# A fused attention and mixing kernel: two DMA transposes of 1024 columns for four of 512, in a new order of steps

## The chip, the cores and the metric

The kernel runs on one core of a Trainium2 chip. The core has a matrix engine (TensorE: PE in the profile, with its weight loads PEld), a vector engine (VectorE, DVE), a scalar engine (ScalarE, ACT), GpSimd (POOL) and SyncE (SP), which here only issues DMA transfers. The engines run side by side, each through its own list of instructions in order, and wait for each other through semaphores. PE writes its results to PSUM, which has eight banks of 128 partitions by 2 KB; DVE and ACT read them there.

The metric is the device time of one execution in microseconds (us), as the median over executions. A change under about half a per cent can't be told from none.

## The reference, cut to what matters

```
B, H, S, D = 8, 8, 576, 64        # q, k, v; factor 4
# attention on means of four neighbouring positions, repeated four times
q_d, k_d, v_d = means of 4 along S
out_up = repeat(softmax(q_d k_d^T / 8) v_d, 4)
# attention within a band: |i - j| < 4
out_local = softmax(where(band, q k^T / 8, -1e9)) v
x = (out_up + out_local), heads side by side: (8, 576, 512)
# mixing
theta = x @ w_theta
y = w_tok_r @ (x cos theta) + w_tok_i @ (x sin theta)      # along the 576 positions
u = x + y
out = u + relu(u @ w_ch)
```

Inputs and output are float32. The kernel computes in bfloat16 with float32 sums.

## The kernel before, in words

The eight batches go through the same chain of steps. Each step is a Python generator (`load`, `cast`, `turns`, ...), and each `yield` ends one piece of it. A string `ORDER` of 1178 letters says which generator is advanced next: `L` is the next piece of `load`, `C` of `cast`, `A` of `turns`, and so on, by the table `sequences` at the end of the kernel. This order fixes the order of the instructions on every engine (`pin` ties each instruction to the one before it on its engine). A second string, `BANKS`, names the PSUM bank of each result, and `ENGINES` the engine of each copy that may run on several (a = ACT, v = DVE, p = POOL). Nothing is scheduled at run time: an instruction whose input is late holds up all that stands behind it on its engine. SP's list holds all loads, all DMA transposes and most stores.

A piece is named here by its letter, batch and number: J1.0 is the first piece of `mix` of batch 1. Those that matter below:

- L, C: thirteen loads a batch into a ring of fifteen buffers `st` (four of k, four of q, five of v, each v piece in two transfers), and their casts to bfloat16. l, c: the twenty weight pieces (0 to 3 w_theta, 4 to 9 and 10 to 15 the two halves of w_tok_r and w_tok_i, 16 to 19 w_ch). V, v: w_tok turned on PE into `WT`, in eighteen pieces.
- A, a: q and k turned on PE; d, e: their sums over four positions; U, P, N, Q: pooled attention; S, m, O, i: banded attention; T, t: both added up into `xT`, x with channels on the partitions (`transposes_out`).
- H, h: theta and its cosines and sines (`phases`, `waves`), for positions 0 to 511 in four pieces. G, g, Z, z: the same for the last 64 positions, with a DMA transpose `z<-zT` at the end (`tail_z`).
- X: x turned back on PE, positions on the partitions (`x_turns`), for batches 0 to 5. M: the same by four DMA transposes of 128 x 512 (`x_turns_by_queue`), for batches 6 and 7 (`BY_QUEUE`), into a spare k buffer. y: the products x cos theta and x sin theta into `z` (`products`).
- J, j: the mix along positions, nine matmuls a piece, and u = x + y into `uT` and `ut` (`mix`, `mix_out`). For all but the first batch: four pieces of 512 positions and one of the last 64.
- R: u turned back by DMA transposes of 128 x 1024 (`residual`). K, b: the channel matmuls and the relu; D: stores. F, E, r, Y: these for the last 64 positions, two batches at a time.

Of the kernel before, what the change touches and what calls it, by code (L numbers as in the profile page):

```python
# [28 lines left out]
CH = 2 * STEP  # L29
NCH = 5  # L30
# [5 lines left out]
PG = CH // 4  # L36
KP = 32
HALF = 64

BY_QUEUE = [6, 7]  # L40
# [5 lines left out]
def kernel(  # L46
# [11 lines left out]
    nc = tc.nc  # L58
# [5 lines left out]


    ORDER = (
        "LkLkCLkLLLCLkCLACLkLkClkACLCCkaLlkAAaeCdkaaSedCkLSSsLPCsmLCOmsoPLkpCLOiopULOuoLuLLxicCxCONCNnLinlCno"
        "ClLAliATCnacmCCQAaLaAqOdatlocTSteeTLsXSsTLCidttmPPlcHcClTCptHOLLcHolpimOoHChlGhyCiXyhXUcLhLuuLOoLxiO"
        "yVxgvcoCCSNiLNnZnscLnCAXnQcamCCVOvoqlCCVVvvACcyTaelAVvtiVzVTaVvvltlcTtvAaTlHlTtVdLLdcLccSscCSsHvJVte"
        "LLVvLhVHvvXVyvChCJVvVVLCLvhLGXCvHyVVvXjjvghJjULLPPuZpCCyXuxLmJypJLOjjLOxSLooimCJLCljACsCiCaNnnNmAanC"  # L70
        "JAanQAqjLdOJOoLLLLzLeiajcToCStSTiCTOsLtSHtoLClsTimCHdstChJCCUlLCCjuAThAeutJLaLOaOLmlCjoPXopyCCiiJxjc"
        "OPLpLGcXyogHACiaxdhHNnLeZANhnnJnXLaSCSCysCjXcmCsQCyKKLURuRCKCqLeCdAuLaJLCOzLbxbjLSPsKALpbOoaiPLTLRbm"
        "CCtoJipTCxLAmCaCLNLTjtJnnTAjLNnTanLLJtttOSoJjQsOiCOGqJHCmjgLhoRHoDDiTjDXhCTiLHhCKCXtCeCAtayTZtKFXzCy"
        "yAHbUaRhLuOmoDHXuCHbRhiOyoiOLSDKsTJLteCHxdTChLdLKLKLbLtJoHLhejGiXDLhLjbXgDyCbAaJXmCCRCPSpdLKxLjybyJO"
        "OsPjJpCZCooAiNiaRzKCSsSCsDnnjbUDuKNdEbAunXLnKCCACyJraOaSemmQTbjqJCLTTxetLDCKsoiLOLDjPtpAbaxCJodLLiCt"
        "OOPooHRpDiimhDTNjtnnJmOOHToioKXijbhLCAXJyCayFHNtChCGgDjnXDnHKyQhbXUyuOZSKYqeuRTzxsoEitdJrPmSbJxTpjjs"
        "OotPpTTJitjtTtKJmbOjoDOSsDHoMNinHRNnRnMKnMGhbmQgihJqTOYoOTKMZDjtoHhDiitHyhTyytbTKyEHTFHztJtjMGhJgZjh"
        "MKHJHbMMzyJrKjjKDhbJyhyRKyYDRbJJDJJbjbJKDjjjDjFRjKKKRbDKKbRDbbbbDEKrDDDDbKbYDD"
    )
    BANKS = (  # L80
        "0246024602467206426014261401246250460267154202604624506102504523674230164267104570135732135143602456"
        "2046042607246074267046723450364260542054607240672401762304126416420106245162056245026754670154206704"
        "7203526043676452346730546025260402560423650436204673267402702460412604526301654012367403267406240376"
        "236042726023701247601234572016763274523410576452341076"
    )
    ENGINES = dict(
        C=(
            "aavvpvaavpppvappppapppvppppaapppppppappppappappapppappaapaapaappvppppapvaavaavpvpppppaapaaaaapvv"
            "papppapp"
        ),  # L90
        a="vvaaavaaaaaaaaaaavvaaaaaaaaaaaaa",
        c="vpapppppppppappppvpp",
        q="vvavaaav",
        u="vaavvavaaaavaaaa",
        v="vvvvavvavvavvavvva",
    )


# [30 lines left out]
    def tile_of(name, shape, dt=BF16):  # L129
        return const.tile(shape, dt, name=name)  # L130
# [109 lines left out]
    wth = tile_of("wth", [P, 4, DM])  # L240
# [24 lines left out]
    held = {}  # L265
# [262 lines left out]
    xTs, zs, css = {}, {}, {}  # L528

    def transposes(b):  # L530
        for c in range(NCH):
# [10 lines left out]
                    )  # L542
            yield

    def transposes_out(b):
        xdT = xds.pop(b)
        xT = xTs[b] = rot("xT", [P, 4, S], BF16, 2)
        for c in range(NCH):
            cnt = OWN[2 * c] + OWN[2 * c + 1]
            nc.vector.tensor_tensor(  # L550
                out=xT[:, :, CH * c:CH * c + cnt].rearrange("p e (m j) -> p e m j", j=4),
                in0=held.pop(("xT", b, c))[:, :, 0:cnt].rearrange("p e (m j) -> p e m j", j=4),
                in1=xdT[:, :, PG * c:PG * c + cnt // 4].unsqueeze(3).to_broadcast([P, 4, cnt // 4, 4]),
                op=ALU.add,
            )
            yield

    def phases(b):  # L560
        xT = xTs[b]
        for c in range(4):
            th = held["th", b, c] = one()
            for dc in range(4):
                nc.tensor.matmul(out=th, lhsT=xT[:, dc, P * c:P * c + P], rhs=wth[:, dc, :], start=(dc == 0), stop=(dc == 3))  # L565
            yield
# [9 lines left out]
    csts, zTs = {}, {}  # L576

    def tail_phases(b):
        xT = xTs[b]
        th = held["tt", b] = one()[:, 0:4 * HALF].rearrange("p (e t) -> p e t", e=4)  # L580
        for ec in range(4):
            for dc in range(4):
                nc.tensor.matmul(out=th[:, ec, :], lhsT=wth[:, dc, P * ec:P * ec + P], rhs=xT[:, dc, 512:576],
                                 start=(dc == 0), stop=(dc == 3))
        yield

# [7 lines left out]
    def z_of(b):  # L594
        if b not in zs:
            zs[b] = rot("z", [P, 9, DM], BF16, 2)
        return zs[b]

    def tail_product(b):
        zT = zTs[b] = rot("zT", [P, 4, 2, HALF], BF16, 1)  # L600
        nc.vector.tensor_tensor(
            out=zT, in0=xTs[b][:, :, 512:576].unsqueeze(2).to_broadcast([P, 4, 2, HALF]), in1=csts.pop(b), op=ALU.mult,
        )
        yield

# [4 lines left out]
        yield  # L610

    def x_turns(b):
        xT = xTs[b]
        for c in range(4):
            ps = held["xt", b, c] = one(BF16)[:, 0:DM]
            for dc in range(4):
                nc.tensor.transpose(out=ps[:, P * dc:P * dc + P], in_=xT[:, dc, P * c:P * c + P], identity=ident)  # L617
            yield

    xms = {}  # L620

    def x_turns_by_queue(b):
        spare = rot("k_tm", [P, 2, WR, 2, D], BF16, 2).rearrange("p i r c d -> p (i r c d)")
        xm = xms[b] = spare[:, 0:4 * DM].rearrange("p (c n) -> p c n", c=4)
        for dc in range(4):
            nc.sync.dma_start_transpose(out=xm[:, :, P * dc:P * dc + P], in_=xTs[b][:, dc, 0:512])
            yield

    def products(b):
        for c in range(4):  # L630
            x = xms[b][:, c, :] if b in BY_QUEUE else held.pop(("xt", b, c))
            nc.vector.tensor_tensor(  # L632
                out=z_of(b)[:, 2 * c:2 * c + 2, :], in0=x.unsqueeze(1).to_broadcast([P, 2, DM]),
                in1=css.pop((b, c)), op=ALU.mult,
            )
            yield

# [6 lines left out]
    def pieces(b):  # L644
        if b in BY_HALF:
            return [(dc, 288 * hf, 288) for hf in range(2) for dc in range(4)]
        whole, tail = [(dc, 0, 512) for dc in range(4)], [(None, 512, HALF)]
        return tail + whole if b == B - 1 else whole + tail
# [9 lines left out]
            yield  # L658

    def mix_out(b):  # L660
        xT = xTs[b]
        uT = uTs[b] = rot("uT", [P, 6, S], BF16, 2).rearrange("p a s -> p (a s)")[:, 0:4 * DM].rearrange("p (e t) -> p e t", e=4)
        if b % 2 == 0:
            uts[b // 2] = rot("ut", [P, 4, 2, HALF], BF16, 2)
        ut = uts[b // 2][:, :, b % 2, :]
        for dc, lo, n in pieces(b):
            ps = held.pop(("u", b, dc, lo))
            if dc is None:
                nc.vector.tensor_tensor(out=ut, in0=ps[:, 0:4 * n].rearrange("p (e t) -> p e t", e=4), in1=xT[:, :, lo:], op=ALU.add)
            else:  # L670
                m = min(512 - lo, n)
                nc.vector.tensor_tensor(out=uT[:, dc, lo:lo + m], in0=ps[:, 0:m], in1=xT[:, dc, lo:lo + m], op=ALU.add)  # L672
                if m < n:
                    nc.vector.tensor_tensor(out=ut[:, dc, :], in0=ps[:, m:n], in1=xT[:, dc, 512:], op=ALU.add)
            yield

    def residual(b):
# [78 lines left out]
    def each(steps, n=B):  # L756
# [57 lines left out]
```

## Time and profile before

| What | us |
|---|---|
| median of three executions | 245.51 |
| lowest, highest | 245.32, 246.25 |
| the profiled execution's own time | 243.21 |
| span of its instructions | 241.5 |

The 40 slices of the page show the busy share of each engine in tenths. In the start PE is the least busy of the four, and the DMA engines are full; from about the eleventh slice (60 us) PE is at 9 nearly throughout; the loads end near the 28th.

```profile
PE   1457878798999799999999999999998998999992
PEld 1344745586687356666665466565754474446441
DVE  1698999885799799989888898999977877657463
ACT  4183689679989789865789498746684174330000
POOL 1588986677475746640066412191410000000000
PEclk9999999889999999999999999999999999999999
DMA  6999999999998998999999999998662187349576
```

A busy PE is not PE at its peak: short matmuls and a lower granted clock stretch it. PEclk is the clock that was granted, in tenths.

### The profile page before, as it was taken

Reading aid. Unit: us, or ns where it says so; the run is one execution under the profiler, and the core shown is the slowest. Engines: PE = TensorE matmul, PEld = TensorE weight load, DVE = VectorE, ACT = ScalarE, POOL = GpSimd, SP = SyncE. Lnnn points to the kernel's source line nnn. Section 1 sums busy time; section 2 is a strip of 40 time slices with the busy share of each in tenths; the row PEclk is TensorE's granted clock in tenths of the full one; section 3 lists DMA queues with packets and bytes.
Section 4 is the critical chain, followed back from the end, with each engine's and each line's share of the span. In section 5 each row is a group of like instructions: output and inputs, shape, how many; then the busy total and the mean of one; then the engine's idle time right before and its main releaser. Section 6 shows DMA issues by size and latency. Waiting matters only on the chain.

```text
span 241.5 us, 8125 instructions
## 1 busy us (share of the span) xinstructions
PE 213.1 (88%) x3307; PEld 135.0 (56%) x3344; DVE 194.1 (80%) x385; ACT 150.5 (62%) x218; POOL 93.4 (39%) x165
## 2 busy tenths in 40 slices
PE   1457878798999799999999999999998998999992
PEld 1344745586687356666665466565754474446441
DVE  1698999885799799989888898999977877657463
ACT  4183689679989789865789498746684174330000
POOL 1588986677475746640066412191410000000000
PEclk9999999889999999999999999999999999999999
DMA  6999999999998998999999999998662187349576
GB/s 201 270 222 297 274 187 271 338 220 160 282 259 194 310 273 184 233 267 155 270 274 230 223 251 222 274 240 217 156 83 78 24 132 177 68 103 244 130 227 213
DMA packets 87190, 50.91 MB, mean 211 GB/s; under 512 B 72048, under 2 KB 72304, under 8 KB 87152
## 3 DMA queue, kind: packets, MB, share of 16 engines
q1 hardware_dynamic: 86640, 49.60, 89.8%
q10 hardware_dynamic: 512, 0.79, 0.9%
q8 instruction: 26, 0.43, 0.8%
q14 instruction: 12, 0.10, 0.1%
HBM read 34.11 MB, written 9.44 MB: 180 GB/s over the span
## 4 chain that ended last, share of the span: by engine, by line
PE 61%; DMA 13%; DVE 10%; issue 4%; ACT 4%; SPq 4%; POOL 3%; DVEq 0%; ACTq 0%; POOLq 0%
PE space L656 25%; PE space L699 10%; PE space L565 6%; DMA st<-in_k_dram 4%; PE space L298 4%; DMA st<-in_moe_w_tok_i_dram 3%; PE space L498 3%; DMA st<-in_q_dram 2%; DVE kd L315 2%; PE space L538 2%; PE space L617 2%; DMA z<-zT 2%; PE space L412 2%; PE space L466 1%; PE space L418 1%
## 5 line engine op out<-in xcount | busy, mean ns | idle before, releaser
L656 PE MATMUL space<-WT,z 128*128 128x64 bf16 (+2 forms) x561 | 76.4, 284 | 3.2 <-DMA z<-zT 1.7
L656 PEld LDWEIGHTS <-z 128*128 128x128 bf16 x576 | 38.6, 98 | 31.6 <-DMA z<-zT 2.7
L672 DVE TENSOR_TENSOR uT<-space,xT 128x512 bf16<-128x512 f32 (+2 forms) x36 | 22.5, 626 | 12.6 <-PE space L656 12.3
L565 PE MATMUL space<-wth,xT 128*128 128x512 bf16 x115 | 31.1, 380 | 1.1 <-issue 0.3
L699 PE MATMUL space<-wch,uT 128*128 128x512 bf16 (+1 forms) x124 | 30.8, 372 | 0.5 <-issue 0.2
L572 ACT ACTIVATE cs<-space,pihc 128x512 bf16<-128x512 f32 x32 | 22.2, 695 | 13.5 <-PE space L565 9.5
L518 DVE TENSOR_TENSOR tmp<-space,rl 128x512 bf16<-128x512 f32 x40 | 26.9, 680 | 1.4 <-PE space L538 0.9
L125 POOL CAST k_tm<-st 128x576 bf16<-128x576 f32 x19 | 14.0, 739 | 34.8 <-DMA st<-in_k_dram 34.7
L550 DVE TENSOR_TENSOR xT<-space,xdT 128x464 bf16<-128x464 f32 (+1 forms) x40 | 24.4, 627 | 2.4 <-PE space L538 2.3
L478 ACT ACTIVATE pm<-space 128x1024 bf16<-128x1024 f32 (+1 forms) x24 | 20.5, 881 | 9.2 <-PE space L466 8.7
L315 DVE TENSOR_REDUCE kd<-kT 128x290 bf16<-128x1160 bf16 x16 | 21.4, 1350 | 0.0
L713 DVE SCALAR_TENSOR_TENSOR osb<-space,ur 128x512 f32<-128x512 f32 x28 | 19.0, 684 | 2.3 <-PE space L699 1.3
L125 POOL CAST v_w<-st 128x512 bf16<-128x512 f32 x21 | 13.6, 656 | 16.7 <-DMA st<-in_v_dram 14.4
L573 ACT ACTIVATE cs<-space 128x512 bf16<-128x512 f32 x32 | 19.3, 603 | 0.0
L298 PE MATMUL space<-ident,k_tm 128*128 128x128 bf16 x144 | 12.6, 241 | 7.4 <-ACT k_tm L125 5.9
L399 ACT ACTIVATE pd<-space 128x864 bf16<-128x864 f32 (+1 forms) x16 | 12.2, 771 | 10.5 <-PE space L380 6.4
L699 PEld LDWEIGHTS <-uT 128*128 128x128 bf16 x132 | 12.0, 98 | 11.5 <-issue 0.5
L125 POOL CAST q_tm<-st 128x576 bf16<-128x576 f32 x18 | 12.5, 702 | 15.0 <-DMA st<-in_q_dram 14.1
L332 POOL TENSOR_TENSOR two<-qT 128x576 f32<-128x576 bf16 x14 | 16.6, 1188 | 3.5 <-ACT qT L125 3.2
L632 DVE TENSOR_TENSOR z<-space,cs 128x1024 bf16<-128x1024 bf16 x24 | 16.2, 681 | 2.1 <-ACT cs L573 1.2
L125 ACT COPY kT<-space 128x1152 bf16<-128x1152 bf16 x14 | 15.7, 1122 | 3.1 <-PE space L298 3.1
L125 ACT COPY qT<-space 128x1152 bf16<-128x1152 bf16 x13 | 14.6, 1125 | 4.2 <-PE space L298 3.9
(95 smaller groups left out, 376.2 us busy)
## 6 DMA issues: line engine op xcount, KB each, us to landing
st<-in_v_dram SPq DMA_DIRECT2D x80, 128.0 KB, 5.3
st<-in_k_dram SPq DMA_DIRECT2D x32, 288.0 KB, 5.5
st<-in_q_dram SPq DMA_DIRECT2D x32, 288.0 KB, 5.6
out_dram<-osb SPq DMA_DIRECT2D x28, 256.0 KB, 4.4
st<-in_moe_w_tok_r_dram SPq DMA_DIRECT2D x6, 216.0 KB, 6.3
st<-in_moe_w_tok_i_dram SPq DMA_DIRECT2D x6, 216.0 KB, 7.1
st<-in_moe_w_theta_dram SPq DMA_DIRECT2D x4, 256.0 KB, 6.4
st<-in_moe_w_ch_dram SPq DMA_DIRECT2D x4, 256.0 KB, 5.3
```

The costliest lines, as they stand in the source:

```text
L125: copies[next(engines[step])](**operands)
L298: nc.tensor.transpose(out=ps[:, P * r:P * r + P], in_=(k_tm if what == "k" else q_tm)[:, i, r, :, :], identity=ident)
L315: nc.vector.tensor_reduce(out=kd[:, hs, :, 0:PG].rearrange("p e g m -> p (e g) m"), axis=AX.X, op=ALU.add, in_=kT[:, hs, :].rearrange("p e ...
L478: nc.scalar.activation(out=pm.rearrange("p e c j w -> p e (c j w)"), in_=held.pop(("S", b, u))[:, :, 0:4 * W * n], func=AF.Exp, scale=SCL)
L518: nc.vector.tensor_tensor(out=tmp.rearrange("p g (j d) -> p g j d", d=D), in0=held.pop(("loc", b, c))[:, :, :, 0:D], in1=rls.pop((b, c)).u ...
L550: nc.vector.tensor_tensor(out=xT[:, :, CH * c:CH * c + cnt].rearrange("p e (m j) -> p e m j", j=4), in0=held.pop(("xT", b, c))[:, :, 0:cnt ...
L565: nc.tensor.matmul(out=th, lhsT=xT[:, dc, P * c:P * c + P], rhs=wth[:, dc, :], start=(dc == 0), stop=(dc == 3))
L572: nc.scalar.activation(out=cs[:, 0, :], in_=th, func=AF.Sin, bias=pihc, scale=1.0)
L573: nc.scalar.activation(out=cs[:, 1, :], in_=th, func=AF.Sin, bias=0.0, scale=1.0)
L656: nc.tensor.matmul(out=ps[:, n * i:n * i + n], lhsT=z[:, j, P * d:P * d + P], rhs=WT[:, j, lo:lo + n], start=(j == 0), stop=(j == 8))
L672: nc.vector.tensor_tensor(out=uT[:, dc, lo:lo + m], in0=ps[:, 0:m], in1=xT[:, dc, lo:lo + m], op=ALU.add)
L699: nc.tensor.matmul(out=ps, lhsT=uT[:, dc, P * c:P * c + P], rhs=wch[:, dc, cols], start=(dc == 0), stop=(dc == 3))
```

## The change: a dense xT for batches 6 and 7, two transfers for four, and a new order

`xT` becomes a pair of views, made by a new function `x_of`. For batches 6 and 7 the first 512 positions of the four channel groups lie densely behind each other, followed by the last 64 of each; for the others the tile is as before and the views are slices of it. Two channel groups can then go through one DMA transpose of 128 x 1024, so `x_turns_by_queue` issues two where it issued four. The result lies by channel group first, so the products read it, and are written, through views with a channel group and 128 columns apart. The last piece of `transposes_out` of these two batches is split at position 512 into two additions. `ORDER`, `BANKS` and `ENGINES` are replaced as a whole: 1174 letters, four M pieces fewer, the same other pieces.

```
+    def x_of(b):
+        t = rot("xT", [P, 4 * S], BF16, 2)
+        if b in BY_QUEUE:
+            return [t[:, 4 * i:4 * i + 4 * n].rearrange("p (e t) -> p e t", e=4) for i, n in ((0, DM), (DM, HALF))]
+        t = t.rearrange("p (e t) -> p e t", e=4)
+        return [t[:, :, 0:DM], t[:, :, DM:], t]
+
     def transposes_out(b):
         xdT = xds.pop(b)
-        xT = xTs[b] = rot("xT", [P, 4, S], BF16, 2)
+        xTs[b] = x_of(b)
         for c in range(NCH):
             cnt = OWN[2 * c] + OWN[2 * c + 1]
...
+            for i, lo, n in [(0, CH * c, cnt)] if c < NCH - 1 else [(0, CH * c, DM - CH * c), (1, 0, HALF)] if b in BY_QUEUE else [(2, CH * c, cnt)]:
...
     def x_turns_by_queue(b):
         spare = rot("k_tm", [P, 2, WR, 2, D], BF16, 2).rearrange("p i r c d -> p (i r c d)")
-        xm = xms[b] = spare[:, 0:4 * DM].rearrange("p (c n) -> p c n", c=4)
-        for dc in range(4):
-            nc.sync.dma_start_transpose(out=xm[:, :, P * dc:P * dc + P], in_=xTs[b][:, dc, 0:512])
+        xm = xms[b] = spare[:, 0:4 * DM].rearrange("p (e c n) -> p e c n", e=4, c=4)
+        for dc in (0, 2):
+            nc.sync.dma_start_transpose(out=xm[:, dc:dc + 2].rearrange("p e c n -> p (e c) n"),
+                                        in_=xTs[b][0][:, dc:dc + 2, :].rearrange("p e t -> p (e t)"))
             yield
 
     def products(b):
         for c in range(4):
-            x = xms[b][:, c, :] if b in BY_QUEUE else held.pop(("xt", b, c))
+            x = xms[b][:, :, c, :] if b in BY_QUEUE else held.pop(("xt", b, c)).rearrange("p (e n) -> p e n", n=P)
             nc.vector.tensor_tensor(
-                out=z_of(b)[:, 2 * c:2 * c + 2, :], in0=x.unsqueeze(1).to_broadcast([P, 2, DM]),
-                in1=css.pop((b, c)), op=ALU.mult,
+                out=z_of(b)[:, 2 * c:2 * c + 2, :].rearrange("p r (e n) -> p r e n", n=P),
+                in0=x.unsqueeze(1).to_broadcast([P, 2, 4, P]),
+                in1=css.pop((b, c)).rearrange("p r (e n) -> p r e n", n=P), op=ALU.mult,
             )
             yield
```

Two stretches of the order, with the letters of the list above. The part in which w_tok is loaded (l), cast (c) and turned (V), and the mix of batch 0 (J) begins, before and after:

```
before  ...datlocTSteeTLsXSsTLCidttmPPlcHcClTCptHOLLcHolpimOoHChlGhyCiXyhXUcLhLuuLOoLxiOyVxgvcoCCSNiLNnZnscLnCAXnQcamCCVOvoqlCCVVvv...
after   ...qtCATlAtLaOtdelaSeToLSciltsscCXLLPLCPCLHmpplhTOLCtOoLmcHCHoiCLCyihlOUOLGLLhugouxxiAaXNcoHClZNnnyXnCCclylnhXSiysQCCqCAlcAcTAatVTlLcvl...
```

and the last steps:

```
before  ...jjjDjFRjKKKRbDKKbRDbbbbDEKrDDDDbKbYDD
after   ...DjDDjRFJjJbjYJJjKEjDKRKKKbKRrbKbRbbbDYDDKbDDDDbD
```

On the engines, `ENGINES` moves copies: of the eight first casts of k and q of batch 0 two q and one k leave DVE for POOL and ACT. ACT's list has eighteen table loads where it had sixteen: the steps that use the exponential and those that use the sine alternate once more.

More of the change, by code (lines that the diff above doesn't have):

```diff
@@ L543, in transposes @@
             yield
+    def x_of(b):
[4 more added lines that the diff above has]
+        return [t[:, :, 0:DM], t[:, :, DM:], t]
     def transposes_out(b):
         xdT = xds.pop(b)
-        xT = xTs[b] = rot("xT", [P, 4, S], BF16, 2)
+        xTs[b] = x_of(b)
         for c in range(NCH):
             cnt = OWN[2 * c] + OWN[2 * c + 1]
[L550 to L555, printed above, removed]
+            ps = held.pop(("xT", b, c))
+            for i, lo, n in [(0, CH * c, cnt)] if c < NCH - 1 else [(0, CH * c, DM - CH * c), (1, 0, HALF)] if b in BY_QUEUE else [(2, CH * c, cnt)]:
+                at = lo + DM * (i == 1) - CH * c
+                nc.vector.tensor_tensor(
+                    out=xTs[b][i][:, :, lo:lo + n].rearrange("p e (m j) -> p e m j", j=4),
+                    in0=ps[:, :, at:at + n].rearrange("p e (m j) -> p e m j", j=4),
+                    in1=xdT[:, :, (CH * c + at) // 4:(CH * c + at + n) // 4].unsqueeze(3).to_broadcast([P, 4, n // 4, 4]),
+                    op=ALU.add,
+                )
             yield
     def phases(b):
-        xT = xTs[b]
+        xT = xTs[b][0]
         for c in range(4):
@@ L582, in tail_phases @@
             for dc in range(4):
-                nc.tensor.matmul(out=th[:, ec, :], lhsT=wth[:, dc, P * ec:P * ec + P], rhs=xT[:, dc, 512:576],
+                nc.tensor.matmul(out=th[:, ec, :], lhsT=wth[:, dc, P * ec:P * ec + P], rhs=xt[:, dc, :],
                                  start=(dc == 0), stop=(dc == 3))
@@ L601, in tail_product @@
         nc.vector.tensor_tensor(
-            out=zT, in0=xTs[b][:, :, 512:576].unsqueeze(2).to_broadcast([P, 4, 2, HALF]), in1=csts.pop(b), op=ALU.mult,
+            out=zT, in0=xTs[b][1].unsqueeze(2).to_broadcast([P, 4, 2, HALF]), in1=csts.pop(b), op=ALU.mult,
         )
@@ L668, in mix_out @@
             if dc is None:
-                nc.vector.tensor_tensor(out=ut, in0=ps[:, 0:4 * n].rearrange("p (e t) -> p e t", e=4), in1=xT[:, :, lo:], op=ALU.add)
+                nc.vector.tensor_tensor(out=ut, in0=ps[:, 0:4 * n].rearrange("p (e t) -> p e t", e=4), in1=xt, op=ALU.add)
             else:
@@ L673, in mix_out @@
                 if m < n:
-                    nc.vector.tensor_tensor(out=ut[:, dc, :], in0=ps[:, m:n], in1=xT[:, dc, 512:], op=ALU.add)
+                    nc.vector.tensor_tensor(out=ut[:, dc, :], in0=ps[:, m:n], in1=xt[:, dc, :], op=ALU.add)
             yield
```

52 lines of the change are left out of this document (26 added, 26 removed).

## The prediction

> **What bounds the kernel now.** I read the page first: which engine is full, and where.
>
> ```profile
> span 241.5 us, 8125 instructions
> PE 213.1 (88%) x3307; PEld 135.0 (56%) x3344; DVE 194.1 (80%) x385; ACT 150.5 (62%) x218; POOL 93.4 (39%) x165
> ```
>
> PE is the fullest engine, with 28.4 us idle. The view by stretches says where; its columns are start:end, length, then busy us and instructions of PE, PEld, DVE, ACT and POOL, the granted clock, the DMA share and GB/s.
>
> ```profile
> 0.00:20.00 20.00, 7.11 (x146) 5.46 (x148) 12.87 (x37) 9.09 (x11) 10.20 (x47) 1.00 0.93 234
> 20.00:40.00 20.00, 17.51 (x355) 11.82 (x346) 18.47 (x37) 14.70 (x21) 16.32 (x26) 1.00 1.09 255
> 40.00:46.00 6.00, 4.25 (x99) 3.27 (x95) 5.09 (x14) 4.83 (x9) 3.76 (x7) 1.00 1.04 325
> 46.00:50.00 4.00, 3.43 (x51) 3.27 (x51) 3.07 (x9) 2.40 (x3) 2.66 (x4) 0.59 1.31 253
> 50.00:60.00 10.00, 9.18 (x168) 6.87 (x168) 7.28 (x15) 9.00 (x13) 7.78 (x11) 0.99 1.01 195
> ...
> 100.00:120.00 20.00, 19.74 (x376) 13.23 (x381) 17.67 (x36) 12.96 (x18) 5.30 (x8) 1.00 1.20 225
> ...
> 200.00:210.00 10.00, 8.76 (x63) 4.51 (x63) 7.21 (x13) 4.00 (x8) 0.00 (x0) 1.00 0.61 134
> ```
>
> Until 60 us the DMA engines are full (shares 0.93 to 1.31) and PE starves. Behind that PE hardly idles. The timeline of PE after 62 us (start, length, work, and in brackets the idle time before it and what ended it) has these waits of more than 0.3 us, and no others:
>
> ```profile
> 82.31 0.39 PE L656 MATMUL space<-WT,z 128*128 128x512 bf16 x1 [1.06 <-DMA z<-zT]
> 84.25 0.68 PE L298 MATMUL space<-ident,q_tm 128*128 128x128 bf16 x9 [0.33 <-ACT q_tm L125]
> 182.76 0.39 PE L656 MATMUL space<-WT,z 128*128 128x512 bf16 x1 [0.66 <-DMA z<-zT]
> 205.69 0.36 PE L538 MATMUL space<-ident,tmp 128*128 128x116 bf16 x4 [1.19 <-DVE xT L550]
> ```
>
> They add up to 3.24 us, which caps what any new order can win behind the start. The fourth belongs to the step that the change rewrites: DVE could not take the next xT because it stood before a product, waiting for x turned by DMA. SP's timeline and the group's idle time show it:
>
> ```profile
> 190.84 1.86 SPq L626 DMA_TRANSPOSE k_tm<-xT  x1
> 195.49 2.58 SPq L626 DMA_TRANSPOSE k_tm<-xT  x2
> 200.26 1.29 SPq L626 DMA_TRANSPOSE k_tm<-xT  x1
> L632 DVE TENSOR_TENSOR z<-k_tm,cs 128x1024 bf16<-128x1024 bf16 x8 | 5.2, 686 | 4.3 <-DMA k_tm<-xT 2.9 <-issue 1.4
> ```
>
> **The yardstick for the new order.** The order is written out, so each step has a place: the PE work that stands ahead of it, summed with the prices of the chain of waits (start, us, work):
>
> ```profile
> 131.34 0.21 PE space L538 x4
> 131.55 1.94 PE space L656 x9
> 133.49 0.86 PE space L565 x4
> 139.09 0.47 PE space L583 x16
> 140.00 0.50 PE space L298 x9
> ```
>
> and likewise for the rest; both orders hold 206.9 us of it, the same matmuls. Three places show how far PE lags behind its work: work 22.6 (V0.4) at 49.59 us, 27.8 (J0.0) at 55.36, 34.5 (J0.2) at 62.28. The lag is 27.0, 27.6, 27.8 us, and from there constant: the start decides 28 of the 34.6 us that the span has over the work (241.5 - 206.9), and what a change does to the lag at about 60 us it does to the end, but for the four waits.
>
> ```profile
> 49.59 0.81 PE L274 MATMUL space<-ident,uT 96*128 96x96 bf16 x9
> 55.36 1.26 PE L656 MATMUL space<-WT,z 128*128 128x288 bf16 x9 [0.72 <-ACT pm L478]
> 62.28 1.26 PE L656 MATMUL space<-WT,z 128*128 128x288 bf16 x9
> ```
>
> **The change part by part.** *Two transfers for four.* Issues of L626 (four of 512 columns) and of the residual's 1024-column form, from the tile views; then the medians to landing:
>
> ```profile
> L626 SPq DMA_TRANSPOSE k_tm<-xT x8: 1192/1268/2277, 190.8 to 213.0; - x8
> L681 SPq DMA_TRANSPOSE ur<-uT x17: 1188/1384/2742, 95.3 to 231.0; - x17
> ur<-uT SPq DMA_TRANSPOSE x17, 4.5
> k_tm<-xT SPq DMA_TRANSPOSE x8, 3.4
> ```
>
> SP spends 4 x 1.27 = 5.1 us on a batch now and 2 x 1.38 = 2.8 us then. Each transfer lands later (4.5 for 3.4 us), but in the new order the last one for batch 6 stands at PE work 168.4 and its first product at 176.7: 8.3 us for 4.5. Before, 170.9 and 172.6: 1.7 us for 3.4. In SP's queue it is behind two stores whose relu is done by then. So the 2.9 us of DVE's wait goes, and PE's 1.19 us. Given back in part: between T7.3 and J6.0 stand 4.3 us of PE work plus six matmuls (1.3), and DVE has there three xT pieces, two relus and four products, nine operations of 0.63 to 0.69 and one more of 0.42 for the split piece, 6.2 us less what they overlap: some 0.5 us. Net -0.7; bounds -1.19 and +0.5 (the wait stays in another form).
>
> *The split last piece* of xT, for two batches: 48 and 64 columns of four rows (192 and 256 elements) instead of 112. The nearest forms are 224 and 256 elements of L672 and L669, so at most 0.42 us of DVE is added to each batch; it is in the sum above. *The products' views* now have four dimensions, for all batches. L601 has such a view already:
>
> ```profile
> L672 DVE TENSOR_TENSOR uT<-space,xT 128x224 bf16<-128x224 f32 x4 | 1.6, 388 | 0.1
> L669 DVE TENSOR_TENSOR ut<-space,xT 128x256 bf16<-128x256 f32 x7 | 2.9, 418 | 1.0 <-PE space L656 1.0
> ...
> L601 DVE TENSOR_TENSOR zT<-xT,cst 128x512 bf16<-128x512 bf16 x8 | 3.5, 442 | 0.6 <-ACT cst L591 0.6
> L486 DVE TENSOR_TENSOR pm<-pm,band 128x512 bf16<-128x512 bf16 x8 | 3.3, 415 | 0.6 <-ACT pm L478 0.6
> L518 DVE TENSOR_TENSOR tmp<-space,rl 128x512 bf16<-128x512 f32 x40 | 26.9, 680 | 1.4 <-PE space L538 0.9
> ```
>
> L601 takes 0.03 us more than L486's flat form of its size: 32 x 0.03 = 1 us of DVE at most, spread over a DVE with 47 us idle: nothing. The far bound, the rate of L518 (512 elements in 680 ns), would be +0.65 us for each of 32, 21 us of DVE.
>
> *The order, at the start.* More first casts go to POOL and ACT, DVE has two q casts and one k cast fewer (0.75 us each, below), and copies kT out before its last memsets. The reduces that hold up the first pooled scores then start some 2 us sooner. I price that gain at nothing, because a DMA stands behind it: V0.1 to V0.8 need w_tok pieces 4 to 9, and the new order loads six more pieces of k and q of batch 2 ahead of them.
>
> ```profile
> L125 DVE CAST q_tm<-st 128x576 bf16<-128x576 f32 x4 | 3.0, 749 | 5.8 <-DMA st<-in_q_dram 5.8
> ```
>
> ```profile
> 38.59 0.61 POOL L125 CAST v_w<-st 128x512 bf16<-128x512 f32 x1 [0.81 <-DMA st<-in_v_dram]
> ...
> 44.00 1.27 POOL L125 CAST uT<-st 96x576 bf16<-96x576 f32 x2 [1.02 <-DMA st<-in_moe_w_tok_i_dram]
> 50.10 0.67 POOL L125 CAST q_tm<-st 128x576 bf16<-128x576 f32 x1 [0.46 <-DMA st<-in_q_dram]
> 55.51 1.27 POOL L125 CAST uT<-st 96x576 bf16<-96x576 f32 x2 [0.34 <-DMA st<-in_moe_w_tok_i_dram]
> ```
>
> Before, those six landed by 50.1 and the tok pieces by 44.6; the set is the same, so now the tok piece is last, at about 50.1, is cast by 50.8, and V0.1 (work 22.5) cannot start earlier: lag 28.3, against 27.0 at the same work. The second gate: V0.10 (work 31.1) needs the last tok piece, which landed at about 56.1 and now stands behind two more pieces of v. One is 256 KB at the 195 GB/s of that stretch, 1.34 us: 58.8, cast by 59.5, lag 28.4 against 27.7. The gates say +1.3 and +0.7; I take +1.0. Bounds: -2 (the early gain arrives whole) and +2.5 (POOL casts three pieces of batch 2 first).
>
> *The order, behind it.* z of batch 1: its transfer had landed 1.06 us late; its product moves from work 36.8 to 33.8, seven loads fewer are ahead of it in SP's queue, and J1.0 moves only from 51.4 to 49.7: -1.06. The q turn at 84.25 (A4.0, A4.1) moves from 53.9 and 54.6 to 55.1 and 60.6, so its loads have 1 to 6 us more: -0.33. z of batch 5: more distance (147.4 to 151.5) but a residual transfer and a store ahead of it: 0. ACT gets two more table loads (sin, exp and back in batches 3 and 4), 1.28 us each by the row below; ACT is idle for 7 us between 100 and 120 us: 0, at most +1.3.
>
> ```profile
> L478 ACT ACT_TABLE_LOAD x4 | 5.1, 1283 | 0.2
> ```
>
> *The end.* R7's three transfers still hang on the last pieces of uT, and the last relus and stores are the same: 0.
>
> **The sum.** 243.21 us is the profiled execution's own time (span 241.5). 243.21 + 1.0 - 1.06 - 0.33 - 0.7 = 242.1. The median shown is 2.3 above that execution: **244.4 us**, 0.4% faster. Half a per cent, 1.2 us, is about what a measurement here can tell from no change.
>
> **The rivals.** *The gates don't bind* (start 0 or better) and all four waits go: 245.5 - 3.24 = 242.3. For: DVE's freed time at the start. Against: DMA shares of 1.0 all the way to 60 us.
>
> *Slower: the clock falls at the gate.* PE's granted clock was 0.59 from 46 to 50 us, after six us at 71% busy (4.25 of 6.00): 4 x 0.41 = 1.6 us. The new order leaves 7.0 us of work between U1.0 (15.5, which needs the v piece that landed by 38.6, cast 0.6 later at 39.2, or some 0.5 sooner with one load fewer ahead) and V0.1 (at 50.8), so PE is some 58% busy there (7.0 of 12.1). A second such fall behind the gate, with the gate at its upper bound and the whole gain on the waits (2.1): 245.5 + 2.5 + 1.6 - 2.1 = 247.5. It makes the kernel slower once gate and clock cost over 2.1 us together. The Trainium skill, page "TensorE: Matmul & The Clock Gate", section "What's actually happening", says that the clock is halved after an idle window of about 3.4 us. By that rule alone PE would have to stand still to lose its clock; this trace lost it with no such gap, so the trace disagrees and the rival is likelier than the rule makes it.
>
> *No change:* the waits go and others of their size come, 245.5.
>
> *Slower: the products lose their rate*, 21 us of DVE, of which DVE's 47 idle us hide perhaps half: 255. L601 speaks against it.
>
> **How the numbers follow.** Forecast 0.45 (its own range 243.2 to 245.6; 0.20 of it below 244.3), gates don't bind 0.18, no change 0.07, clock at the gate 0.25, slow products 0.05. Faster by over 0.5%: 0.20 + 0.18 = 0.38; within: 0.25 + 0.07 = 0.32; slower: 0.30. The range 241.3 to 248.5 leaves out the slow products and the edges of two rivals.
>
> **What would show it.** Right: no wait of DVE on k_tm<-xT; SP issues of some 1.4 us, four in all; PE's first wait for WT's pieces near 50 us; no z wait at J1.0. Wrong: J0.0 starting before 55 us (the gates were no gates) or after 58.5; a granted clock under 0.8 past 52 us; products over 0.75 us; new waits of PE behind 62 us of more than 2 us in sum.

## The result, and the profile after

| | changed kernel | kernel before, same chip | ratio, 95% interval |
|---|---|---|---|
| first comparison, median | 242.25 us (4 executions) | 245.47 us (4) | 0.9857 [0.9828, 0.9886] |
| once more, median | 243.09 us (12) | 245.48 us (29) | 0.9907 [0.987, 0.9944] |
| profiled execution, own time | 241.83 us | 243.21 us | |
| its span | 240.1 us | 241.5 us | |

The change makes the kernel faster, by 1.4% in the first comparison and 0.9% in the second, where 0.4% was forecast. Between the profiled executions it is 1.4 us. The ratios leave out executions that were disturbed.

The head of the page, and the view by stretches (columns as in the prediction: busy us and instructions of PE, PEld, DVE, ACT, POOL, the clock, the DMA share, GB/s):

```profile
span 240.1 us, 8125 instructions
PE 211.8 (88%) x3311; PEld 134.9 (56%) x3344; DVE 195.2 (81%) x381; ACT 153.7 (64%) x222; POOL 95.6 (40%) x169
```

```profile
46.00:50.00 4.00, 1.90 (x33) 1.57 (x30) 2.93 (x6) 1.83 (x3) 2.42 (x4) 1.00 1.07 233
50.00:52.00 2.00, 1.12 (x18) 0.85 (x22) 1.37 (x3) 1.24 (x4) 1.63 (x4) 0.88 1.27 212
52.00:54.00 2.00, 2.00 (x87) 1.78 (x87) 1.45 (x3) 1.33 (x5) 1.92 (x3) 0.50 1.06 247
54.00:56.00 2.00, 1.95 (x27) 1.27 (x19) 1.26 (x2) 1.85 (x3) 2.00 (x4) 0.77 1.50 181
...
100.00:140.00 40.00, 38.58 (x559) 23.48 (x566) 36.36 (x65) 32.81 (x46) 13.99 (x21) 1.00 1.14 240
```

PE is busy 1.90 of the 4 us from 46 to 50, where it had 3.43 before: it waits for loads. The clock then falls to 0.50, later than before (46 to 50 us). PE's timeline shows the waits, and POOL's what ends them (in brackets the idle time and what ended it):

```profile
48.76 0.68 PE L298 MATMUL space<-ident,q_tm 128*128 128x128 bf16 x9 [1.93 <-POOL q_tm L125]
49.28 0.29 PE L274 MATMUL space<-ident,uT 96*128 96x96 bf16 x3
49.41 0.37 PE L538 MATMUL space<-ident,tmp 128*128 128x116 bf16 x4
49.62 0.21 PE L274 MATMUL space<-ident,uT 96*128 96x96 bf16 x1
50.29 0.22 PE L274 MATMUL space<-ident,uT 96*128 96x96 bf16 x1 [0.47 <-POOL uT L125]
51.10 0.90 PE L274 MATMUL space<-ident,uT 96*128 96x96 bf16 x13 [0.59 <-POOL uT L125]
...
58.80 1.27 PE L669 MATMUL space<-WT,z 128*128 128x288 bf16 x9
```

```profile
49.57 1.47 POOL L125 CAST uT<-st 96x576 bf16<-96x576 f32 x2 [0.16 <-DMA st<-in_moe_w_tok_i_dram]
```

The longest wait, 1.93 us, is for a q piece of batch 2, one of the six that the new order loads first. V0.1 (50.8 forecast) has three matmuls, at 49.62, 50.29 and 51.10; the last two are each held up by the cast of a w_tok piece. J0.0 starts at 58.80, where it had 55.36. Behind 62 us these are PE's waits of more than 0.3 us:

```profile
82.49 0.24 PE L348 MATMUL space<-v_w,pu 128*32 128x128 bf16 x4 [1.56 <-ACT v_w L125]
124.56 0.35 PE L594 MATMUL space<-xT,wth 128*128 128x64 bf16 x6 [1.05 <-issue]
```

Both are new, and the four of before are gone. The first is U3.0, pooled v of batch 3, behind the last piece of v. The second stands in the middle of G3.0, after ten of its sixteen matmuls, and no semaphore ended it; what it is comes further down. The rewritten transfers and the products, from the view of the tile:

```profile
L644 DVE TENSOR_TENSOR z<-k_tm,cs x8: 681/683/685, 205.5 to 218.0; 128x1024 bf16<-128x1024 bf16 x8
L637 SPq DMA_TRANSPOSE k_tm<-xT x4: 1232/1298/1724, 191.9 to 209.0; - x4
...
DMA to landing us min/median/max: 3.1/3.8/5.0
```

Four issues of 1.30 us, 3.8 us to landing (4.5 forecast), products at 0.683 us (0.686 before), and no wait of DVE on them. At the end, the chain that ended last, first of the changed kernel and then of before (start, us, work; DVEq issues the last store):

```profile
235.61 1.02 DVE st L726 x2
236.63 0.33 DVEq L822
```

```profile
236.28 1.02 DVE st L713 x2
237.31 0.33 DVEq L809
```

From there to the end of the span it is 3.1 us (240.1 - 236.96) and was 3.9 (241.5 - 237.64).

**Where the time went.** A yardstick like the prediction's, PE's lag behind the PE work ahead of a step, tells it step by step. One price in the prediction's was wrong: a group of 64 matmuls of the banded scores is two pieces, and had been counted for each, so that the total is 200.4 us and not 206.9. With that mended (each step's place is the start of its first weight load in the trace):

| PE work ahead, us | before | after | x_in_old | half_tok | u3_later |
|---|---|---|---|---|---|
| 40 | 30.1 | 31.5 | 30.0 | 30.9 | 31.2 |
| 50 | 32.5 | 33.1 | 33.3 | 30.8 | 31.8 |
| 60 | 32.9 | 33.3 | 33.7 | 31.0 | 33.9 |
| 85 | 33.3 | 33.6 | 34.4 | 31.9 | 34.2 |
| 90 | 33.3 | 34.7 | 34.4 | 32.2 | 37.0 |
| 165 | 35.0 | 35.6 | 36.0 | 33.6 | 38.6 |
| 170 | 36.3 | 35.6 | 36.0 | 33.6 | 38.6 |
| the last step | 36.4 | 35.7 | 36.1 | 33.6 | 38.7 |
| PE's end to the span's end | 4.4 | 3.7 | 4.5 | 3.7 | 3.7 |

(The last three are experiments, below.) After minus before: +1.4 at the gate, -1.1 from there to 85, +1.1 at G3.0, -0.8 from there to 165, -1.3 between 165 and 170, where before stood at the x of batch 6, and -0.7 behind PE's end: -1.4.

### The profile page after: what moved, and what is told of

Read it like the earlier page. It is cut to its first block, busy times and chain, and to the rows that moved or that the text cites. A ratio compares the mean times of both kernels' runs of the same rounds, so it can differ in the third digit from the quotient of the medians.

```text
span 240.1 us, 8125 instructions
## 1 busy us (share of the span) xinstructions
PE 211.8 (88%) x3311; PEld 134.9 (56%) x3344; DVE 195.2 (81%) x381; ACT 153.7 (64%) x222; POOL 95.6 (40%) x169
## 4 chain that ended last, share of the span: by engine, by line
PE 70%; DMA 13%; POOL 8%; SPq 3%; issue 3%; ACT 1%; DVE 1%; DVEq 0%; POOLq 0%; ACTq 0%
PE space L669 27%; PE space L712 11%; PE space L576 10%; DMA st<-in_v_dram 5%; PE space L298 4%; DMA st<-in_moe_w_tok_i_dram 3%; PE space L538 3%; POOL full L146 3%; DMA st<-in_q_dram 3%; PE space L498 2%; DMA st<-in_k_dram 2%; PE space L628 2%; PE space L466 2%; PE space L594 2%; PE space L718 1%
## 5 line engine op out<-in xcount | busy, mean ns | idle before, releaser
L669 PE MATMUL space<-WT,z 128*128 128x512 bf16 (+2 forms) x568 | 76.1, 285 | 0.7 <-issue 0.2
L712 PE MATMUL space<-wch,uT 128*128 128x512 bf16 (+1 forms) x123 | 31.3, 373 | 0.5
L561 DVE TENSOR_TENSOR xT<-space,xdT 128x464 bf16<-128x464 f32 (+3 forms) x42 | 24.5, 605 | 4.7 <-PE space L538 4.5
L125 POOL CAST v_w<-st 128x512 bf16<-128x512 f32 x22 | 14.1, 642 | 18.1 <-DMA st<-in_v_dram 6.2
L125 POOL CAST q_tm<-st 128x576 bf16<-128x576 f32 x21 | 14.2, 682 | 15.7 <-DMA st<-in_q_dram 15.6
L125 POOL CAST k_tm<-st 128x576 bf16<-128x576 f32 x19 | 12.8, 675 | 14.6 <-DMA st<-in_k_dram 13.6
L125 ACT COPY qT<-space 128x1152 bf16<-128x1152 bf16 x14 | 15.7, 1124 | 4.2 <-PE space L298 3.5
L298 PE MATMUL space<-ident,k_tm 128*128 128x128 bf16 x144 | 12.1, 236 | 5.7 <-ACT k_tm L125 5.6
L576 PEld LDWEIGHTS <-xT 128*128 128x128 bf16 x128 | 11.2, 98 | 10.1 <-issue 0.3
L125 ACT COPY kT<-space 128x1152 bf16<-128x1152 bf16 x12 | 13.5, 1121 | 4.5 <-PE space L298 4.4
```

Source lines behind the costliest of these rows:

```text
L125: copies[next(engines[step])](**operands)
L298: nc.tensor.transpose(out=ps[:, P * r:P * r + P], in_=(k_tm if what == "k" else q_tm)[:, i, r, :, :], identity=ident)
L561: nc.vector.tensor_tensor(out=xTs[b][i][:, :, lo:lo + n].rearrange("p e (m j) -> p e m j", j=4), in0=ps[:, :, at:at + n].rearrange("p e (m ...
L669: nc.tensor.matmul(out=ps[:, n * i:n * i + n], lhsT=z[:, j, P * d:P * d + P], rhs=WT[:, j, lo:lo + n], start=(j == 0), stop=(j == 8))
L712: nc.tensor.matmul(out=ps, lhsT=uT[:, dc, P * c:P * c + P], rhs=wch[:, dc, cols], start=(dc == 0), stop=(dc == 3))
```

## The experiments

The kernel before has medians of 244.8 to 245.5 us on the chips of these runs and spreads over 3 us and more on each, so ratios to it on the same chip count. All intervals are at 95%.

### The two kernels again

No edit: the kernel before, and the changed kernel, as they are.

> The kernel before, unchanged, with the span and granted clock of each execution. Theory A (its profiled execution at 243.2 us was a lucky one): executions at 245.3 to 246.3 us have a lower mean granted clock than 0.993, and a new profile shows a longer span, by about 2 us, from a clock that falls more often in the first 60 us. Theory B (the profiled execution is typical and timed ones carry 2 us outside the span): spans near 241.5 us at 245.4 us.

> The changed kernel once more, on the chip of the other experiments, for its spread. Theory (the start waits for the loads; each stretch of 3.4 us of half clock in the first 60 us that does not fall into such a wait costs 1 to 1.5 us): median 242 to 242.6, single times from 240 to 245, the profiled span within 1.5 us of 240.1 and lower by 1 to 1.5 for each stretch of half clock fewer. Rival (the two-and-a-bit us between the profiled executions' difference of 1.4 and the medians' of 3.2 are a gain that only unprofiled runs have): median 242.2 with a spread under 1 us.

Measured: before again 244.88 us (12 executions, 243.48 to 246.5), ratio 1.0021 [0.9982, 1.0061]; the changed kernel again 243.09 (12, 241.79 to 246.7), 0.9907 [0.987, 0.9944]. In every execution the time is 1.6 to 1.8 us over the span, so the spread is in the span. The profiled executions: 244.68 for before, where the first had been 243.21, and 241.88 for the changed one, where the first had been 241.83. The second of before has its clock down for longer:

```profile
46.00:50.00 4.00, 2.12 (x21) 1.81 (x20) 2.50 (x6) 1.58 (x2) 2.01 (x3) 0.66 1.74 223
50.00:54.00 4.00, 3.78 (x40) 3.73 (x40) 2.21 (x6) 2.38 (x4) 3.72 (x6) 0.50 0.71 182
```

So the execution from which the prediction was made was a fast one: none of those 12 was below 243.48. A median over it of 2.3 us is a draw and no property of the kernel; here it is 0.2 us. In the changed kernel's second execution the clock fell twice in the start, in the first once, and the spans agree within 0.1 us: a count of such falls does not give the time.

### The x change alone, and the order alone

x_in_old is the old order, with the new `x_of`, `transposes_out`, `x_turns_by_queue` and `products`; of the four M places of each of the two batches the first two stay. four_in_new is the new order with the old functions, each M doubled.

```
-  "...nRnMKnMGhbmQ...tjMGhJgZjh"  "MKHJHbMMzyJ..."      # ORDER of before
+  "...nRnMKnGhbmQ...tjMGhJgZjhMK" "HJHbzyJ..."          # x_in_old
```

> The x change alone, in the old order of all other steps; the two transfers stand at the first two of the four places. Theory A (each part gives what the sum says): DVE's wait of 2.9 us on the transfers goes, PE's wait of 1.19 us with it: 1.2 us less than before, 244.3 us. Rival (the x change carries the whole gain of 3.2 us): 242.3 us. Rival (a 1024-column transfer costs what two of 512 do): no change, 245.5 us.

> The new order with the old x: four transfers of 512 columns at the places of the two. SP spends 2.3 us more on each batch. Theory A: for batch 6 there are 11 us between the last transfer and the first product, so nothing; for batch 7 the last one lands some 2 us later, close to its first product: 0 to 0.7 us slower than the changed kernel, 242.3 to 243.0 us. Rival (the order was found for two transfers and needs them): 1.2 us slower or more, 243.5 us and up.

Measured: x_in_old 243.83 us (12 executions), ratio 0.9961 [0.993, 0.9992]; four_in_new 243.56 (6, 239.91 to 247.54), 0.9877 [0.9809, 0.9945], a ratio that rests on three of the six. In x_in_old the lag stays at 36.0 from 165 to 170, where before goes from 35.0 to 36.3. The transfers, in its view of the tile:

```profile
L637 SPq DMA_TRANSPOSE k_tm<-xT x4: 1233/1340/1596, 191.5 to 208.7; - x4
```

The x change alone is worth 0.4%, a microsecond, and PE's wait of 1.19 us is gone from its trace; DVE still waits 1.0 us for the transfers, where it had 2.9. That wait of PE differs between executions of the four transfers in the old order: it is 0.9 us in the second one of before, and 0.2 in warm_old's (below).

The new order hides it without the x change too. In four_in_new's trace DVE never waits for its four transfers, and behind 165 us PE has one wait of more than 0.3 us, of another kind:

```profile
222.37 1.21 PE L656 MATMUL space<-WT,z 128*128 128x64 bf16 x36 [0.44 <-DVE uT L672]
```

So either part alone removes the wait. What the x change adds to the new order the executions can't tell: 0.9877 with four transfers and 0.9907 with two lie within each other's intervals.

### Half of the first w_tok loads

```
-  nc.sync.dma_start(out=t[0:OC], in_=(moe_w_tok_r, moe_w_tok_i)[i][OC * ct:OC * ct + OC, :])
+  n = S // 2 if ct < 3 else 0
+  nc.sync.dma_start(out=t[0:OC, n:], in_=(moe_w_tok_r, moe_w_tok_i)[i][OC * ct:OC * ct + OC, n:])
```

> The changed kernel, but the six transfers of the first half of w_tok bring only the last 288 of 576 columns, so half of their bytes (the other columns hold what the buffer held). Theory A (the tok pieces are the gate of the start, and the lag there goes to the end undiminished): the last of them lands some 2 us sooner, the mix of batch 0 starts 1 to 2 us sooner, and the whole is 1 to 2 us faster than the changed kernel, 240.3 to 241.3 us. Rival (the start is bound by something else, or what is won there is waited for again later): no change, 242.3 us.

This kernel leaves half of the bytes of six pieces out. Measured: 240.09 us (6 executions), ratio 0.9795 [0.9738, 0.9851]; profiled span 238.0, 2.1 below the changed kernel's. By the table, 0.6 of it is there at 40 us of work, 2.3 at 50, and 2.1 at the end. PE no longer waits in V0.1, nor for the q piece ahead of it, nor at U3.0, and POOL casts the w_tok pieces one behind the other without waiting:

```profile
47.67 2.50 POOL L125 CAST uT<-st 96x576 bf16<-96x576 f32 x4
```

What the loads give in the first 80 us arrives at the end nearly whole. But J0.0 starts at 58.23, only 0.6 us sooner, where 1 to 2 were expected, and most of the gain is collected at U3.0, 30 us behind the gate: the loads set the pace up to U3.0, and a gate is where PE notices. Fewer bytes bring every load behind them forward, so the run speaks for the loads as a whole, not for the w_tok pieces alone.

### The end alone

x_and_end_in_old: x_in_old, with F3, E3, r3 and Y3 as early as in the new order.

```
-  "...bJyhyRKyYDRbJJDJJbjbJKDjjjDjFRjKKKRbDKKbRDbbbbDEKrDDDDbKbYDD"
+  "...bJyhyRKyYDRbJJDJJbjbJKDjFjjDjERjKKKRbrDKKbRDYbbbbDKDDDDbKbDD"
```

> The kernel before with the x change (which alone gave 243.8) and with the four last steps of the output path (F3, E3, r3, Y3) moved forward to where the new order has them; the start and the middle are the old ones. Theory (the new order's end is worth 0.7 us because the last stores but three leave earlier): PE's end to the span's end 3.7 us for 4.4, time 243.0 to 243.3. Rival (the end is bound by the last relu and its store, which did not move; the 0.7 us between the profiles came from elsewhere): 243.8, with 4.4 us behind PE's end.

Measured: 243.97 us (12 executions), ratio 0.9962 [0.9928, 0.9996], where x_in_old had 0.9961; behind PE's end 3.9 us, where x_in_old had 4.5. The tail is shorter by 0.5 in this profile as in the new order's, and x_end_warm_old below shows it again (4.0 for 4.5). The medians of two batches of executions don't tell 0.5 us. The profiled execution was a long one (span 243.9) and stood 1.24 us at a place in the start with no releaser, of which more below.

### Matmuls added in the start

If the clock falls because PE has little to do, matmuls that nobody needs keep it up. They go into the bank that the next step overwrites.

```
+    def fill(ap, n):
+        for _ in range(n):
+            nc.tensor.matmul(out=ap, lhsT=ident, rhs=wth[:, 0, :], start=True, stop=True)
...
+            fill(ap[:, 0, :], {(2, 0): 3, (2, 1): 2}.get((b, n), 0))     # warm_old, x_warm_old, x_end_warm_old
+            fill(ap[:, 0, :], {(2, 3): 8}.get((b, n), 0))                # warm_new
+            fill(ap[:, 0, :], {(1, 2): 2, (1, 3): 3, (2, 3): 8}.get((b, n), 0))   # warm_new_early
```

and one or two ahead of two V pieces in each.

> The changed kernel with twelve more matmuls (64 to 128 columns wide weights already in place, 512 columns out) on TensorE in its long waits for the loads: eight ahead of the turn A2.3, two each ahead of V0.1 and V0.2, each into the bank that the step then overwrites. Nothing else differs. Theory (the fall of the clock near 51 us is a matter of how little PE does ahead of it, and costs 1 to 1.5 us): no stretch of half clock from 45 to 60 us, J0.0 as before within 0.5 us or earlier, time 240.8 to 241.6, and less spread. Rival (the gates alone set the start, the clock falls into waits): 242.2 as the changed kernel. Second rival (the added work delays what stands behind it): 243 to 244, with J0.0 later than 59.3.

> The kernel before with seven such added matmuls: three ahead of A2.0, two ahead of A2.1, one each ahead of V0.0 and V0.1. Theory (the fall at 46.7 us costs 1 to 1.5 us): no stretch of half clock from 44 to 52 us and 243.4 to 243.9 where the kernel before has 244.8 on this chip. Rival (the fall costs nothing, the loads set the start): 244.8. Second rival (added work delays): 245.5 to 246.5.

> The kernel before with the x change (alone 0.9961 of before) and with the seven added matmuls ahead of A2.0, A2.1, V0.0 and V0.1 (alone 0.9888 of before); the order is the old one. Theory (the two act on different waits, one at the last batches' x and one at the clock in the loads' stretch, so their gains add): ratio 0.985, some 241.2 where the kernel before has 244.8. Rival (the added matmuls' gain in that run was at the last batches too, where its step was 0.4 us for the 1.3 of before, so it is the same microsecond): ratio 0.988 to 0.989.

> As x_warm_old, with the last steps of the output path (F3, E3, r3, Y3) forward as in the new order. Theory (PE's end to the span's end falls by 0.5 as it did in x_and_end_in_old, and here no spread hides it): 0.5 us below x_warm_old, some 240.7, with at most 4.0 us behind PE's end. Rival (the steps moved forward cost PE as much earlier): within 0.2 us of x_warm_old.

> The changed kernel with the twelve matmuls of warm_new and five more ahead of the turns A1.2 (two) and A1.3 (three), at 28 to 30 us, ahead of the place (31 to 34 us) where the clock fell in warm_new and in the changed kernel's second execution. Theory (the spread and the missing gain of warm_new were these earlier falls): no half clock from 25 to 60 us, median 241 to 241.8 and most times within 1 us of each other, as warm_old has them. Rival (in this order the loads set the start whatever the clock is): 243 to 244 with the spread of warm_new.

| | median us (executions) | ratio | without the matmuls |
|---|---|---|---|
| warm_old | 242.21 (6) | 0.9888 [0.9851, 0.9925] | 1 |
| x_warm_old | 243.47 (12) | 0.9958 [0.9922, 0.9993] | 0.9961 |
| x_end_warm_old | 242.64 (12) | 0.9936 [0.99, 0.9972] | 0.9962 |
| warm_new | 243.79 (12) | 0.9937 [0.9903, 0.9972] | 0.9907 |
| warm_new_early | 244.34 (12) | 0.9942 [0.9892, 0.9993] | 0.9907 |

warm_old alone has the lowest time of these; with the x change added it is 0.9958, no lower than the x change alone, so the six executions of warm_old can't be taken for a gain of the matmuls. The theory that falls of the clock make the spread fell here: the clock of x_warm_old was 1.000 in 9 of 12 executions, and seven of these alone reach from 241.15 to 244.5 us, with the other two above that. Its profiled execution has no fall in the start (the stretches from 46 to 54 us and the core's span and mean are below), and a span like the changed kernel's, which had one:

```profile
46.00:50.00 4.00, 3.73 (x67) 2.97 (x66) 3.68 (x11) 2.81 (x4) 2.55 (x5) 1.00 1.30 273
50.00:54.00 4.00, 3.30 (x92) 2.47 (x95) 3.39 (x5) 2.27 (x4) 3.52 (x5) 1.00 0.98 247
```

```profile
core 0: 240.1 us, clock 1.000
```

In warm_new the added work did keep the clock at 1.00 from 45 to 60 us; 6.8 us of half clock came at 32.7 us instead. Its lag at 60 us of work was 32.6 (33.3 in the changed kernel), and at 90 us 34.4 (34.7): what PE gained it spent in the next wait.

### U3.0 behind the phases

U3.0 and its first copy go behind H2.2, with other banks.

```
-  "...loLloUjHLHiidLuCCHmAlaLhJhTuL..."
+  "...loLlojHLHiidLCCHUumAlaLhJhTuL..."
```

> The changed kernel with U3.0 (pooled v of batch 3), on which TensorE waits 1.56 us at 82.5 for the last piece of v, moved behind H2.2, that is behind 2.6 us of TensorE's work that needs no load; its copy u3.0 goes with it, and it has other banks. Theory (the wait of one step for one load is worth its length where other work is at hand): no wait of TensorE at L348 after 70 us, the step of the lag from work 85 to 90 at most 0.4 us where the changed kernel has 1.1, and the end 0.8 to 1.2 us earlier at the same arrival of the loads: span 239 for 240.1, ratio to before 0.984 to 0.987 where the changed kernel had 0.9907 and 0.9857. Rival (the loads set this stretch whatever stands in it: A4.0, right behind, waits for k of batch 4, which lands 0.6 to 1.3 us behind v): PE waits the same time at A4.0 or J1.1, time as the changed kernel.

Measured: 244.41 us (12 executions), ratio 0.995 [0.9905, 0.9996], no gain, and a profiled span of 243.1. Neither expectation came. The wait at U3.0 went, as the theory said: at 50 us of work the lag is 31.8 (33.1). PE then waits for ACT. In both kernels ACT's list has the copy of U3.0 ahead of the sines and cosines that X2.0 and J1.2 need. With U3.0 behind H2.2, ACT stands 2.37 us until it may copy, and begins the first of them at 85.84 us, where the changed kernel had 85.07:

```profile
88.13 0.38 PE L628 MATMUL space<-ident,xT 128*128 128x128 bf16 x4 [0.57 <-ACT cs L584]
89.20 2.10 PE L669 MATMUL space<-WT,z 128*128 128x512 bf16 x9 [0.68 <-ACT cs L584]
...
126.88 0.36 PE L594 MATMUL space<-xT,wth 128*128 128x64 bf16 x7 [2.79 <-issue]
```

At 60 us of work the lag is 33.9, above the changed kernel's 33.3. And the stop in G3.0 is 2.79 us instead of 1.05. Moving one step past a wait moves its copy on the other engine too.

### What stops PE in G3.0

This is read from the traces; no run was made for it. In all seven executions of the new order PE stops there, and in two of them at another step, because 12 and 17 matmuls were added ahead (L720 and L506 are K1.1 and O4.3 there; the lines are from warm_new, warm_new_early and half_tok, one each):

```profile
123.63 0.60 PE L720 MATMUL space<-wch,uT 128*128 128x512 bf16 x2 [1.56 <-issue]
```

```profile
125.15 0.22 PE L506 MATMUL space<-v_w,pm 64*64 64x65 bf16 x3 [2.32 <-issue]
```

```profile
122.08 0.35 PE L595 MATMUL space<-xT,wth 128*128 128x64 bf16 x6 [0.23 <-issue]
```

Counted from the start, the stop is behind the 1882nd weight load each time: in G3.0 without added matmuls; 12 matmuls further back in the program with 12 added, in the middle of K1.1; 17 further back with 17, in O4.3. So it hangs on the count of PE's instructions and not on data. The page lists a DMA queue of its own for them:

```profile
q8 instruction: 26, 0.43, 0.8%
```

That is 26 packets of 16 KB (q14, the other one, has 12 of 8). In the trace's DMA records the last of them ahead of the stop ended, against PE's next weight load:

| | packet ends | load 1883 | between | PE stood |
|---|---|---|---|---|
| after | 123.3 | 124.56 | 1.3 | 1.05 |
| after, again | 123.3 | 124.64 | 1.3 | 1.09 |
| warm_new | 122.4 | 123.63 | 1.2 | 1.56 |
| four_in_new | 125.0 | 126.47 | 1.5 | 1.60 |
| warm_new_early | 123.8 | 125.14 | 1.3 | 2.32 |
| half_tok | 120.6 | 122.08 | 1.5 | 0.23 |
| u3_later | 125.4 | 126.88 | 1.5 | 2.79 |
| before | 118.9 | 123.54 | 4.6 | 0 |
| x_in_old | 120.0 | 124.67 | 4.7 | 0 |
| x_warm_old | 119.7 | 122.91 | 3.2 | 0 |

PE goes on 1.2 to 1.5 us behind the packet whenever it stood, and in the old order the packet is there 3 to 5 us early. Count and packets together speak for PE waiting for its own instructions. It is not shown: no run took the packets away or moved them. Why the packet comes late in the new order is open: the DMA share from 100 to 140 us is 1.14 there, and was 1.17 before.

## Why the prediction was right, and where it was not

**The sign and the range held; the gain was two to three times the forecast 0.4%.** Three of the four signs of an error that the prediction named came all the same (J0.0 past 58.5 us, the clock under 0.8 past 52, new waits of over 2 us), so that the time came out as near as it did is in part luck. Term by term, against the lags:

- *Start, "I take +1.0".* +1.4 at 40 us of work; the last two of V0.1's three matmuls came at 50.29 and 51.10 us for 50.8. The loads do bind, so the rival *The gates don't bind* is out, though its price of 242.3 is what the first comparison measured (242.25). J0.0 at 58.80 is past the 58.5 that was named (58.40 in the second execution), so the start took 0.3 to 0.4 more than priced. The longest wait there is for the q piece and not for w_tok. half_tok speaks for the loads behind it, but moves J0.0 by 0.6 us only.
- *"-1.06" for z of batch 1 and "-0.33" for A4.* Together -1.1 by the lags. Both waits went, but 1.56 us came at U3.0, which the prediction did not look at. A gain is left because before lost 3.2 us of lag between 40 and 85 us of work, of which those two waits are 1.39; the changed kernel loses 2.1, of which U3.0 is 1.56. What the rest of before's 3.2 was is not assigned; by it the lag was not, as the prediction had it, constant but for the four waits.
- *z of batch 5, "0".* That wait of 0.66 us is gone; with what is around it the stretch from 90 to 165 gave -0.8.
- *Two transfers, "-0.7".* -1.3: the wait went whole, and the 0.5 that was to be given back to DVE's nine operations was not. x_in_old loses the wait too, and so does four_in_new, with four transfers: either alone removes it, so the runs don't split the -1.3 between the x change and the order.
- *The views and the split piece, "nothing".* Right: 0.683 us a product.
- *The end, "0".* -0.7. The last relus and stores are the same, but F, E, r and Y of the last two batches are ahead of them in the new order, and the last lines of PE's and DVE's lists are shorter by them. x_and_end_in_old shows 0.5 of it in its profile. The diff had it, in the two last stretches that were quoted.
- *Two more table loads of ACT, "0, at most +1.3".* No wait of PE that ACT's table loads end is among those behind 62 us; the +1.1 at G3.0 is most likely PE's instructions, a wait of a kind that no term held.

So -1.1 was forecast and -1.4 came between the profiled executions, with errors of +0.4, +0.3, +1.1, -0.8, -0.6 and -0.7 that nearly cancel. The step that failed most is the last one, "The median shown is 2.3 above that execution". It was carried over whole, and the changed kernel's median is 0.4 (first comparison) and 1.2 us (second) above its profiled execution: this is why the medians differ by more than the profiles. The profiled execution of before was a fast one, 1.5 us faster than its next, so the terms were sized on an execution that lacked some of what the usual ones lose. By which waits those lose it stays open; the clock alone, as shown, does not order them.

*The clock at the gate*, the rival for slower: the fall came, 0.50 from 52 to 54 us, below the 0.8 that was named, and the kernel was not slower. The price of 1.6 us is not borne out: in warm_new the fall did not come at this place (though 6.8 us of half clock came earlier), and PE was 0.3 us ahead at 90 us of work. What PE did in the 3.4 us ahead of the fall at 51.5 stands in its timeline above: but for one row of 0.37 us (L538) these are transposes (L298, L274; `nc.tensor.transpose` in the code), with no wait over 1.93 us.

The prediction set the trace against one rule of the Trainium skill, page "TensorE: Matmul & The Clock Gate", section "What's actually happening": an idle window of some 3.4 us halves the clock. The same page says in the section "Part 4: PE-mode transpose" that transposes do not count as work in the same way. Both together would fit the fall at 51.5, but other traces speak against them as its cause. In x_in_old PE does nothing but transposes (L298, L446) and one such row of 0.37 us from 25.2 to 29.4 us, and the clock stays at 1.00:

```profile
25.94 0.68 PE L298 MATMUL space<-ident,q_tm 128*128 128x128 bf16 x9
26.72 0.37 PE L538 MATMUL space<-ident,tmp 128*128 128x116 bf16 x4
...
27.55 0.67 PE L298 MATMUL space<-ident,k_tm 128*128 128x128 bf16 x9
28.79 0.68 PE L298 MATMUL space<-ident,q_tm 128*128 128x128 bf16 x9 [0.57 <-POOL q_tm L125]
```

In warm_new it falls at 32.7 us, behind 3.4 us in which PE was busy for 2.34, with only 0.40 of transposes. What makes it fall stays open.

*No change* and *slow products* are out.

*New waits behind 62 us of more than 2 us in sum* were named as a sign of an error: 1.56 + 1.05 = 2.6. They were there, and smaller than the four old waits and the shorter tail (3.24 + 0.7).

No version tried is faster than the changed kernel by more than the intervals, but half_tok, which leaves work out.

## What to carry to other kernels

Where loads set the pace, a wait that an order removes can come back, as 1.56 us did here, at the next step that needs a load: price the stretch up to the last such step, and look for that step by name. Take the yardstick from two executions at least before terms of 0.3 us are summed: here the two differ by 1.5. And a step that is moved on one engine takes its copies along on the others; u3_later lost on ACT what it won on PE.

## What the hardware showed beyond that

PE stood 0.23 to 2.79 us, most likely for its own instructions, always behind the same number of weight loads (1882), and went on 1.2 to 1.5 us after a 16 KB packet of the instruction queue had ended. The profile calls it "issue", in the middle of a group of matmuls that wait for nothing. The same sign stands in the start behind 733 loads: 1.24 us in x_and_end_in_old at 56.86, 0.56 in u3_later, 0.27 in half_tok, each 1.4 to 1.6 us behind a packet. Packets of that queue come from 15.8 to 222 us of the changed kernel, so they come while the program runs.

Half clock came in the start of most profiled executions, in stretches of 3.4 or 6.8 us that began at 31 to 35 or 47 to 52 us; PE had not stood still ahead of them (1.90 of 4 us busy in the changed kernel, 4.25 of 6 before). Each profiled execution had none (x_in_old, warm_old, x_warm_old), one, or two, 10.2 us together in four_in_new. The time did not follow them.
